# Channel loop of a gated attention and state-space kernel: short-lag sums moved to the step after their DRAM skew write, vector work reordered

## Chip, cores and metric

One core of a Trainium2 chip runs the whole program: the forward pass and all gradients of one layer. The metric is device microseconds for one execution, the median of several runs. Engines by short name: PE (matrix), DVE (vector), ACT (scalar), POOL (GpSimd) and SP, whose queue issues every DMA of this kernel. Each engine works through its own instructions in order and waits on semaphores for the others.

## Reference

The layer mixes two branches of a token sequence `x` (2048 tokens, 576 channels) with a gate of one number per token:

```python
g = _sigmoid((x * gate_w).sum(-1, keepdims=True))
a = _A_ref(x, A_wqkv, A_wo)                 # attention, 32 heads
b = _B_ref(x, B_A_re, ..., B_Dskip)         # state-space convolution
return g * a + (1 - g) * b
```

The second branch convolves every channel with a kernel of its own, made of 128 complex exponentials (shortened):

```python
logdA = dt * A                              # [D, N]
P = jnp.exp(logdA[:, :, None] * l[None, None, :])
K = jnp.einsum("dn,dnl,dn->dl", Cc, P, dB).real
y = irfft(rfft(u, 2L) * rfft(K, 2L))[:L] + u * Dskip
```

What is returned is the output and the gradients to all inputs, of which the state-space parameters need sums over all pairs of tokens by lag.

## The kernel before

**Stages.** The first 240 us project queries, keys and values; then comes attention with its gradients; from 2500 us the output projections' gradients; from 2890 to 4304 us the *channel loop*, the only part that changes; the last 175 us assemble outputs.

**Channel loop.** 576 channels are taken in 18 blocks of 32 (`CB`), each in two halves of 16 (`GS`). A sequence of 2048 is cut into 16 chunks (`NB`) of 128 positions. A step `i` of the loop works on several blocks at once: it prepares block `i+1`, scans and finishes block `i`, computes the close part of the convolution for block `i-1`, and in a side chain makes the short-lag sums of block `i+2`. The pieces, by the names used below:

- `ex`: on ACT, the exponential of the decay (tile `ab`), from a `phase` matmul on PE. `kk`, `ff`, `sn`: the angle. `kk` rounds the phase on ACT (the rounding pieces, four to a half), `ff` on DVE (L871) takes the fraction, `sn` makes three ACT passes of sine and square over a half. `prod` (L884, L885) multiplies on DVE to the tile `E1e`, and SP transposes it by DMA into `E1n`.
- `uv`: 32 matmuls with `E1e` against `RX`, the block's columns of input and gradient; ACT copies four pieces to `UV`. `RX` is loaded and scaled for two blocks at a time (`load_rx`, `prep_rx`), in even steps.
- `scan` (L910 to L920): 14 dependent steps of three DVE operations each on the chunk states `HG`; `casts` copies them on ACT; `rw1` (L936) and `rw2` (L942, L943) scale them into `Rw`; `ybp` is 64 matmuls from `Rw` to the far part of the output, copied by ACT to `ydi`, and the first column of the convolution kernel to `K0c`.
- `kp`: PE transposes `K0c`, ACT casts it, SP writes it to `Kp_d` in DRAM. `t0`, a step later: `T0w` reads it back as shifted copies (one buffer, 512 KB), 16 matmuls give `tps` in PSUM, and `tps` plus `ydi` is the output tile `yd`.
- `pairs` (L975 to L993): products of `UV` with the states on DVE, combined to three pairs of `rr` (one buffer), each pair added up by 30 or 28 matmuls against an identity; `sums` copies the result from the PSUM tile `misc`.
- Short-lag sums: `m_load` loads `xs` and `gyp` and makes seven copies of `xs` shifted by partitions; `m_mask` (L797, L799) masks them on DVE; `m_part` multiplies on PE into `psM` (one PSUM buffer that `tps` shares) and ACT copies to `mst`, which SP writes to `Md_d` in DRAM; `m_sum` reads `Md_d` back askew into `skw` (two buffers, four loads a block) and adds up on PE; `m_fin` copies to `RX`.

**What sets the order.** On PE, ACT, DVE and POOL the instructions stand as the loop's Python text emits them, call after call (a manual schedule). SP's DMAs are placed by the framework's scheduler, so that SP's order is seen in the built program. The phase matmuls have three PSUM buffers, `kk` one buffer, `RX` and `UV` two.

Of the kernel before, what the change touches and what calls it, by code (L numbers as in the profile page):

```python
# [20 lines left out]
def build(tc, aps, dbg_aps=None, stages=("s1", "attn", "post", "s4", "final")):  # L21
# [39 lines left out]
    with ExitStack() as gctx:  # L61
# [646 lines left out]
        if "s4" in stages:  # L708
# [13 lines left out]
            with ExitStack() as ctx:  # L722
# [37 lines left out]
                for u in range(2):  # L760
                    m_u = pc.tile([P, 4, MW], F32, name=f"mst{u}")
                    nc.vector.memset(m_u[:, :, P:MW], 0.0)
                    mst2.append(m_u)
                misc = pps.tile([P, 512], F32, tag="misc", name="misc")
# [180 lines left out]
                def ybp(b, h):  # L945
                    B_ = blk(b)
                    if h == 0:
                        B_["ydi"] = pw.tile([P, 2 * NS, CB], F32, tag="ydi", name="ydi")
                        B_["K0c"] = pw.tile([P, CB], F32, tag="K0c", bufs=2, name="K0c")
# [8 lines left out]
                    nc.scalar.copy(B_["ydi"][:, :, hs], yp[:, 1:, :])  # L958
# [9 lines left out]
                def pairs(b):  # L968
                    B_ = blk(b)
                    UV, hR, gR = B_["UV"], B_["hR"], B_["gR"]  # L970
                    pq = [pw.tile([P, 2, 2, 2, NS, CB], BF, tag=tg, name="pq") for tg in ("wA", "wB")]
                    pA, pB, pC, pD = pq[0][:, 0], pq[0][:, 1], pq[1][:, 0], pq[1][:, 1]

                    def pr(o, a_, hh):
                        nc.vector.tensor_tensor(o.rearrange("p a b n c -> p a b (n c)"),  # L975
                                                a_.rearrange("p b n c -> p b (n c)").unsqueeze(1).to_broadcast([P, 2, 2, NS * CB]),
                                                hh.rearrange("p a n c -> p a (n c)").unsqueeze(2).to_broadcast([P, 2, 2, NS * CB]), op=A.mult)

                    pr(pA, UV[:, :, CV0:CV0 + NS, :], hR)
                    pr(pB, UV[:, :, CV1:CV1 + NS, :], hR)  # L980
                    pr(pC, UV[:, :, CU1:CU1 + NS, :], gR)
# [3 lines left out]
                    nc.vector.tensor_tensor(pB, pB, pC, op=A.add)  # L985
                    for u, (pt_, n) in enumerate(((pA, NS), (pB, NS), (pD, NS - 1))):
                        rr = pw.tile([P, 2, NS, CB], BF, tag="rr", name="rr")
                        nc.vector.tensor_tensor(rr[:, 0, 0:n], pt_[:, 0, 0, 0:n], pt_[:, 1, 1, 0:n], op=A.subtract)
                        nc.vector.tensor_tensor(rr[:, 1, 0:n], pt_[:, 0, 1, 0:n], pt_[:, 1, 0, 0:n], op=A.add)
                        for ri in range(2):  # L990
                            o = (2 * u + ri) * CB
                            for k in range(n):
                                mm(misc[:, o:o + CB], lhsT=ident_bf, rhs=rr[:, ri, k, :], start=(k == 0), stop=(k == n - 1))  # L993
# [4 lines left out]
                def t0(b, h):  # L998
# [14 lines left out]
                    nc.scalar.copy(yd[:, :, 0, o0:o0 + GS], tps[:, :, 0, :])  # L1013
                    ydi = B_["ydi"].rearrange("p (a k) c -> p a k c", a=2)
                    nc.vector.tensor_tensor(yd[:, :, 1:NB, o0:o0 + GS], tps[:, :, 1:NB, :], ydi[:, :, :, h * GS:(h + 1) * GS], op=A.add)
# [11 lines left out]
                m_part(0, 1)  # L1027
                m_sum(0)
                m_fin(0)
                for i in range(-1, NBLK + 1):  # L1030
                    cur = 0 <= i < NBLK
                    nx = i + 1 < NBLK
                    mb = i + 2 if 1 <= i + 2 < NBLK else None
# [4 lines left out]
                    if cur:  # L1038
                        scan(i, 0, 4)
                    if nx:  # L1040
                        ff(i + 1, 0, 0); kk(i + 1, 0, 2)
                    if cur:
                        scan(i, 4, 7)
                    if nx:
                        ff(i + 1, 0, 1); kk(i + 1, 0, 3)
                    if cur:
                        scan(i, 7, 10)
                    if nx:
                        ff(i + 1, 0, 2)
                    if cur:  # L1050
                        scan(i, 10, 12)
# [15 lines left out]
                    if mb is not None and mb % 2 == 0:  # L1067
                        load_rx(mb // 2)
# [235 lines left out]
```

## Time and profile before

| what | us |
|---|---|
| runs: median of 3 (lowest, highest) | 4484.52 (4476.69, 4487.67) |
| the profiled execution | 4480.74 |
| its span | 4479.0 |
| attention and gradients, 240 to 2500: PE busy | 2214.8 of 2260 |
| channel loop, 2890 to 4304: DVE, ACT, PE busy | 834.4, 596.3, 518.4 of 1414 |
| `HG` cast (L910), once a step: first and last start | 2969.7, 4248.0 |

The profile is of one execution. A row of its timeline has the start and duration in us, the engine, the line, the operation, the tiles (out, then in), a count, and in brackets the engine's idle time before the row with what ended it. A row of the waits has the engine and line that waited, the engine and tile waited for, and then the total in us, the number of times and the longest. Where a helper emits an instruction (`mm`, L30), the line is the helper's, and the tile tells the place.

### The profile page before, as it was taken

The numbers are of one execution on the slowest core, as the hardware profiler recorded it, in microseconds if no ns is written. First come the engines' busy times: TensorE is split into PE (matmuls) and PEld (weight loads), VectorE is DVE, ScalarE is ACT, GpSimd is POOL, SyncE is SP. The second block draws the span as 40 slices with busy tenths as digits, with TensorE's granted clock in tenths as the row PEclk, the third lists the DMA queues.
The fourth block names the chain that finished last, engine by engine and source line by source line (L and its number), as shares of the span: only waits on it lengthen the run. The fifth ranks groups of instructions, "written<-read, shape, count | busy, mean of one in ns | idle before, by whom it ended". The sixth has DMA issues, their size and how long they took to land. (4 is left out here: it accounts for less than half of the span.)

```text
span 4479.0 us, 64906 instructions
## 1 busy us (share of the span) xinstructions
PE 3291.8 (73%) x24562; PEld 1166.9 (26%) x24562; DVE 2927.3 (65%) x5146; ACT 2933.1 (65%) x5376; POOL 21.8 (0%) x45
## 2 busy tenths in 40 slices
PE   8889999999999999999999987833343333343411
PEld 2312222222222222222222223522222222232300
DVE  5437777777677777776777771155656566565668
ACT  5379989899899898998998951154444444444401
POOL 0000000000000000000000000000000000000000
PEclk9855555555555555555555558955555555555555
DMA  7446777777776767777667777643443334243337
GB/s 195 137 111 118 126 136 122 133 129 124 138 120 126 135 122 132 129 125 136 121 122 127 121 146 210 147 80 74 73 79 71 77 66 88 56 82 71 69 114 170
DMA packets 1789270, 521.42 MB, mean 116 GB/s; under 512 B 1702074, under 2 KB 1767684, under 8 KB 1788956
## 3 DMA queue, kind: packets, MB, share of 16 engines
q1 hardware_dynamic: 1788956, 517.27, 59.5%
q8 instruction: 193, 3.16, 0.3%
q14 instruction: 121, 0.99, 0.1%
HBM read 102.10 MB, written 60.96 MB: 36 GB/s over the span
## 5 line engine op out<-in xcount | busy, mean ns | idle before, releaser
L604 DVE TENSOR_TENSOR ds<-ps_P,PT 128x512 bf16<-128x512 f32 x2048 | 1329.6, 687 | 467.7 <-PE ps_P L30 262.6
L595 ACT ACTIVATE PT<-ps_P 128x512 bf16<-128x512 f32 x2048 | 1226.3, 603 | 138.2 <-PE ps_P L30 86.3
L599 ACT ACTIVATE eb<-ps_P 128x512 bf16<-128x512 f32 x2048 | 1237.0, 606 | 19.9 <-PE ps_P L30 19.3
L30 PE MATMUL ps_P<-dOaT,VaT_g 19*128 19x512 bf16 x2048 | 1197.7, 601 | 26.6 <-DMA VaT_g<-VaT_d 25.7
L30 PE MATMUL ps_P<-KaT_g,QaT_g 19*128 19x512 bf16 x2048 | 1166.1, 594 | 7.6 <-ACT PT L595 7.6
L30 PE MATMUL ps_P<-QaT_g,KaT_g 19*128 19x512 bf16 x2048 | 1054.1, 615 | 9.8 <-DMA KaT_g<-KaT_d 5.8
L30 PE MATMUL accO<-PT,Vtok_g 128*32 128x512 bf16 x2048 | 331.5, 631 | 0.0
L30 PE MATMUL accK<-dsT,Qtok_g 128*32 128x256 bf16 x4096 | 315.2, 406 | 1.7 <-DVE dqa L481 0.8
L30 PEld LDWEIGHTS <-KaT_g 19*128 19x128 bf16 x2048 | 135.6, 103 | 690.6 <-issue 664.8
L30 PEld LDWEIGHTS <-VaT_g 19*128 19x128 bf16 x2048 | 197.3, 98 | 434.2 <-issue 404.8
L30 PE MATMUL psM<-xs,gyp 128*32 128x128 bf16 x576 | 42.3, 423 | 339.4 <-DVE xs L799 322.0
L30 PE MATMUL accQ<-ds,Ktok_g 128*32 128x512 bf16 x2048 | 266.9, 620 | 1.2 <-DVE dvacc L464 1.2
L30 PE MATMUL accV<-eb,dOa 128*32 128x512 bf16 x2048 | 266.9, 620 | 0.6 <-DVE dkacc L505 0.6
L871 DVE SCALAR_TENSOR_TENSOR kk<-kk,ph 128x512 f32<-128x512 f32 x144 | 95.1, 684 | 249.5 <-ACT kk L866 249.5
L30 PE MATMUL uvp<-RX,E1e 128*128 128x64 bf16 x1152 | 134.1, 290 | 111.9 <-DVE E1e L885 111.9
L30 PE MATMUL ph<-thr,lrow 3*128 3x512 bf16 x288 | 147.4, 591 | 64.0 <-DVE kk L871 20.7
L30 PEld LDWEIGHTS <-QaT_g 19*128 19x128 bf16 x2048 | 179.0, 100 | 51.6 <-issue 28.0
L481 DVE TENSOR_TENSOR dqa<-dqa,accQ 128x512 f32<-128x512 f32 x224 | 153.8, 687 | 48.9 <-PE accQ L30 48.6
L877 ACT ACTIVATE uk<-kk 128x2048 f32<-128x2048 f32 x36 | 68.8, 1911 | 176.0 <-DVE kk L871 175.9
L903 ACT ACTIVATE UV<-uvp 128x512 bf16<-128x512 f32 x144 | 86.0, 597 | 144.0 <-PE uvp L30 143.8
L464 DVE TENSOR_TENSOR dvacc<-dvacc,accV 128x512 f32<-128x512 f32 x224 | 154.0, 688 | 37.1 <-PE accV L30 19.5
L30 PE MATMUL ybp<-Rw,E1n 128*128 128x31 bf16 x1152 | 72.7, 233 | 134.8 <-ACT ydi L958 94.5
(279 smaller groups left out, 3641.4 us busy)
## 6 DMA issues: line engine op xcount, KB each, us to landing
T0w<-Kp_d SPq DMA_DIRECT2D x36, 512.0 KB
dsT<-ds SPq DMA_TRANSPOSE x512
dqkv_d<-dtk SPq DMA_DIRECT2D x96, 72.0 KB
dqkv_tok<-dqkv_d SPq DMA_DIRECT2D x1, 6912.0 KB
Md_d<-mst SPq DMA_DIRECT2D x144, 36.0 KB
ga_d<-ga_st SPq DMA_DIRECT2D x16, 288.0 KB
dxm_d<-dxm SPq DMA_DIRECT2D x16, 288.0 KB
skw<-Md_d SPq DMA_DIRECT2D x72, 64.0 KB
```

Source lines behind the costliest of these rows:

```text
L30: return nc.tensor.matmul(out, lhsT=lhsT, rhs=rhs, start=start, stop=stop, **kw)
L464: nc.vector.tensor_tensor(a_, a_, acc, op=A.add)
L481: nc.vector.tensor_tensor(U["dqa"], U["dqa"], acc, op=A.add)
L595: nc.scalar.activation(U["PT"][i][:, j, :], ps, ACT.Exp)
L599: nc.scalar.activation(e, ps, ACT.Exp)
L604: nc.vector.tensor_tensor(U["ds"][i][:, j, :], ps, U["PT"][i][:, j, :], op=A.mult)
L871: nc.vector.scalar_tensor_tensor(v_, v_, MAGIC, B_["ph"].pop((h, q)), op0=A.subtract, op1=A.subtract)
L877: nc.scalar.activation(uk, f_, ACT.Sin, scale=0.5 * TWO_PI * SIN_SAFE)
L903: nc.scalar.mul(UV[:, ri, :, c0:c0 + 8], pr, -1.0 if ri == 0 else 1.0)
```

## The change

Five things move; the arithmetic is the same.

1. The side chain of short-lag sums is one step longer. In step `i`, loading, masking and `m_part` are for block `i+3` (`mb`), and `m_sum` with `m_fin` is for block `i+2` (`sb`), whose `Md_d` was written at the end of the step before. Masks stand between the first half's `ybp` work and the second half's products; `m_part` is the last call of a step. Block 1's loading, masks and `m_part` come ahead of the loop.
2. `pairs` is split. `pairs1` (one product, its `rr`) stays; `pairs2` (the other products and sums) follows the second half's `uv`. `rr` has two buffers.
3. `rw1` follows `casts` directly, both `t0` halves come after it, `prep_rx` moves from a step's end to the place behind `t0`; the scan is dealt out as 2, 2, 2, 2 and 6 steps around the `ff`.
4. The third rounding piece of the second half is emitted ahead of `uv`; the fourth comes after the first `ff`, and `rw2` ahead of all four.
5. `ydi` becomes one tile, `ydi0`, with a zero column in front, so that one DVE addition writes `yd` and ACT's copy of column 0 goes.

```diff
+                ydi0 = pc.tile([P, 2, NB, CB], F32, name="ydi0")
+                nc.vector.memset(ydi0[:, :, 0, :], 0.0)
...
-                    nc.scalar.copy(B_["ydi"][:, :, hs], yp[:, 1:, :])
+                    nc.scalar.copy(ydi0[:, :, 1:NB, hs], yp[:, 1:, :].rearrange("p (a k) c -> p a k c", a=2))
...
+                def psum(u, pt_, n):
+                    rr = pw.tile([P, 2, NS, CB], BF, tag="rr", bufs=2, name="rr")
...
+                def pairs1(b):
...
+                    pmul(pq[0][:, 0], UV[:, :, CV0:CV0 + NS, :], hR)
+                    psum(0, pq[0][:, 0], NS)
+
+                def pairs2(b):
...
+                    pmul(pB, UV[:, :, CV1:CV1 + NS, :], hR)
+                    pmul(pC, UV[:, :, CU1:CU1 + NS, :], gR)
+                    nc.vector.tensor_tensor(pB, pB, pC, op=A.add)
+                    psum(1, pB, NS)
...
+                    psum(2, pD, NS - 1)
...
-                    nc.scalar.copy(yd[:, :, 0, o0:o0 + GS], tps[:, :, 0, :])
-                    ydi = B_["ydi"].rearrange("p (a k) c -> p a k c", a=2)
-                    nc.vector.tensor_tensor(yd[:, :, 1:NB, o0:o0 + GS], tps[:, :, 1:NB, :], ydi[:, :, :, h * GS:(h + 1) * GS], op=A.add)
+                    nc.vector.tensor_tensor(yd[:, :, :, o0:o0 + GS], tps, ydi0[:, :, :, h * GS:(h + 1) * GS], op=A.add)
...
+                m_load(1)
+                m_mask(1)
                 m_sum(0)
                 m_fin(0)
+                m_part(1, 0)
+                m_part(1, 1)
                 for i in range(-1, NBLK + 1):
...
-                    mb = i + 2 if 1 <= i + 2 < NBLK else None
+                    mb = i + 3 if i + 3 < NBLK else None
+                    sb = i + 2 if i + 2 < NBLK else None
...
                     if cur:
-                        scan(i, 12, 15)
+                        scan(i, 9, 15)
                         casts(i)
+                        rw1(i)
+                    if sb is not None and sb % 2 == 0:
+                        load_rx(sb // 2)
                     if i >= 1:
                         t0(i - 1, 0)
-                    if mb is not None:
-                        m_mask(mb)
-                        m_part(mb, 0)
-                    if i >= 1:
                         t0(i - 1, 1)
-                    if mb is not None:
-                        m_part(mb, 1)
...
+                    if sb is not None and sb % 2 == 0:
+                        prep_rx(sb // 2)
                     if nx:
                         prod(i + 1, 0)
-                        kk(i + 1, 1, 0); kk(i + 1, 1, 1)
+                        kk(i + 1, 1, 0); kk(i + 1, 1, 1); kk(i + 1, 1, 2)
                         uv(i + 1, 0)
-                    if cur:
-                        rw1(i)
-                    if nx:
-                        ff(i + 1, 1, 0); kk(i + 1, 1, 2)
-                        ff(i + 1, 1, 1); kk(i + 1, 1, 3)
                     if cur:
                         rw2(i)
                     if nx:
+                        ff(i + 1, 1, 0); kk(i + 1, 1, 3)
+                        ff(i + 1, 1, 1)
...
-                        pairs(i)
+                        pairs1(i)
                         kp(i)
+                    if mb is not None:
+                        m_mask(mb)
                     if nx:
                         prod(i + 1, 1)
                         uv(i + 1, 1)
                     if cur:
-                        sums(i)
-                    if mb is not None:
-                        if mb % 2 == 0:
-                            prep_rx(mb // 2)
-                        m_sum(mb)
-                        m_fin(mb)
+                        pairs2(i)
+                    if sb is not None:
+                        m_sum(sb)
+                        m_fin(sb)
                     if i + 2 < NBLK:
                         ex(i + 2, 0)
                         ex(i + 2, 1)
+                    if cur:
+                        sums(i)
+                    if mb is not None:
+                        m_part(mb, 0)
+                        m_part(mb, 1)
```

On **DVE**, in the middle of a step, from the last scan operation to `rw2`, before:

```order
L920 TENSOR_TENSOR HG<-tz 128x4x32
L1015 TENSOR_TENSOR yd<-tps,ydi 128x2x15x16
L797 TENSOR_TENSOR gyp<-gyp,omp 128x512
L799 TENSOR_SCALAR xs<-xs,msk 128x512 x7
L1015 TENSOR_TENSOR yd<-tps,ydi 128x2x15x16
L884 TENSOR_TENSOR E1e<-kk,ab 128x16x128
L885 SCALAR_TENSOR_TENSOR E1e<-uk,ab 128x16x128
L936 TENSOR_TENSOR wa<-HG,par 128x1920
L936 TENSOR_TENSOR wb<-HG,par 128x1920
L871 SCALAR_TENSOR_TENSOR kk<-kk,ph 128x512 x2
L942 TENSOR_TENSOR Rw<-wb,wa 128x960
L943 SCALAR_TENSOR_TENSOR Rw<-wa,wb 128x960
```

and after, in an even step, from the same operation to the `ff`:

```order
L922 TENSOR_TENSOR HG<-tz 128x4x32
L938 TENSOR_TENSOR wa<-HG,par 128x1920
L938 TENSOR_TENSOR wb<-HG,par 128x1920
L1022 TENSOR_TENSOR yd<-tps,ydi_39429 128x32x16 x2
L786 TENSOR_TENSOR RX<-gob,omg_t 128x1024
L788 TENSOR_SCALAR RX<-RX,l1col 128x960
L789 TENSOR_SCALAR RX<-RX,l0col 128x960
L886 TENSOR_TENSOR E1e<-kk,ab 128x16x128
L887 SCALAR_TENSOR_TENSOR E1e<-uk,ab 128x16x128
L944 TENSOR_TENSOR Rw<-wb,wa 128x960
L945 SCALAR_TENSOR_TENSOR Rw<-wa,wb 128x960
L873 SCALAR_TENSOR_TENSOR kk<-kk,ph 128x512 x4
```

The scalings `wa` and `wb` stand ahead of both `yd`, the masks have left this place, `prep_rx` (L786 to L789) has come in ahead of the products, and all four `ff` (L873) follow `rw2`.

On **ACT**, at the end of a step, from the last `UV` pieces of the second half to the first rounding pieces of the next step, before:

```order
L903 ACTIVATE UV<-uvp 128x64x8 x4
L996 COPY SS<-misc 128x6x32
L832 CAST RX<-misc 128x32
L833 ACTIVATE RX<-misc,l0col 128x32
L834 COPY dDs_row<-misc 1x32
L859 ACT_TABLE_LOAD
L859 ACTIVATE ab<-ph 128x512 x8
L866 ACTIVATE kk<-ph,magc 128x512 x4
```

and after:

```order
L905 ACTIVATE UV<-uvp 128x64x8 x4
L834 CAST RX<-misc 128x32
L835 ACTIVATE RX<-misc,l0col 128x32
L836 COPY dDs_row<-misc 1x32
L861 ACT_TABLE_LOAD
L861 ACTIVATE ab<-ph 128x512 x8
L1005 COPY SS<-misc 128x6x32
L812 COPY mst_39425<-psM 128x4x128
L812 COPY mst_39427<-psM 128x4x128
L868 ACTIVATE kk<-ph,magc 128x512 x4
```

`SS` has moved behind the exponentials (`ab`), and the two `mst` copies, which stood in the middle of the step, now come between these and the rounding pieces (`kk`).

On **SP**, from the `Kp_d` write of a block, before:

```order
L966 DMA Kp_d<-KT 32x128
L1008 DMA T0w<-Kp_d 128x16x128
L887 DMA_TRANSPOSE E1n<-E1e 128x32x128
L825 DMA skw<-Md_d 128x1x128 x2
L845 DMA thr<-spl_d 3x2048
L1008 DMA T0w<-Kp_d 128x16x128
L845 DMA thr<-spl_d 3x2048
```

and after, from the second transpose:

```order
L889 DMA_TRANSPOSE E1n<-E1e 128x32x128
L967 DMA Kp_d<-KT 32x128
L1017 DMA T0w<-Kp_d 128x16x128
L827 DMA skw<-Md_d 128x1x128 x2
L815 DMA Md_d<-mst_39425 16x4x144 x4
L815 DMA Md_d<-mst_39427 16x4x144 x4
L793 DMA xs<-in_A_x_dram 128x16x32
L794 DMA gyp<-in_grad_out_dram 128x16x32
L1017 DMA T0w<-Kp_d 128x16x128
L796 DMA xs<-xs 127x512
```

The transpose of the second half now precedes the `Kp_d` write and the first `T0w` load; the two `skw` loads still come behind all three, and the `Md_d` writes, the loads of `xs` and `gyp` and the second `T0w` follow them. The other two `skw` loads of a block stand behind the seven `xs` shifts (here the first of them is the last row).

More of the change, by code (lines that the diff above doesn't have):

```diff
@@ new lines, in psum @@
+                def psum(u, pt_, n):
+                    rr = pw.tile([P, 2, NS, CB], BF, tag="rr", bufs=2, name="rr")
+                    nc.vector.tensor_tensor(rr[:, 0, 0:n], pt_[:, 0, 0, 0:n], pt_[:, 1, 1, 0:n], op=A.subtract)
+                    nc.vector.tensor_tensor(rr[:, 1, 0:n], pt_[:, 0, 1, 0:n], pt_[:, 1, 0, 0:n], op=A.add)
+                    for ri in range(2):
+                        o = (2 * u + ri) * CB
+                        for k in range(n):
+                            mm(misc[:, o:o + CB], lhsT=ident_bf, rhs=rr[:, ri, k, :], start=(k == 0), stop=(k == n - 1))
@@ L969, in pairs @@
+                def pairs1(b):
                     B_ = blk(b)
                     UV, hR, gR = B_["UV"], B_["hR"], B_["gR"]
[L971 to L977, printed above, removed]
@@ L984, in pairs @@
                                                 hR[:, ri, 1:NS, :].unsqueeze(1).to_broadcast([P, 2, NS - 1, CB]), op=A.mult)
[L985 to L993, printed above, removed]
+                    psum(2, pD, NS - 1)
                 def sums(b):
@@ L1038, in build @@
                     if cur:
-                        scan(i, 0, 4)
+                        scan(i, 0, 3)
                     if nx:
@@ L1042, in build @@
                     if cur:
-                        scan(i, 4, 7)
+                        scan(i, 3, 5)
                     if nx:
@@ L1046, in build @@
                     if cur:
-                        scan(i, 7, 10)
+                        scan(i, 5, 7)
                     if nx:
@@ L1050, in build @@
                     if cur:
-                        scan(i, 10, 12)
+                        scan(i, 7, 9)
                     if nx:
```

16 lines of the change are left out of this document (9 added, 7 removed).

## Prediction

> **What bounds the kernel now.** I read the page first (its 40 slices and the granted clock), then a table of windows by stage, then the waits inside the channel loop, then the timeline of two neighbouring steps. The change touches the loop alone, and nothing else in the span of 4479.0 us moves.
>
> ```profile
> span 4479.0 us, 64906 instructions
> 2890.00:4304.00 1414.00, 518.43 (x5490) 356.53 (x5490) 834.41 (x1502) 596.31 (x881) 0.22 (x1) 0.52 0.38 72
> 3583.80:3662.30 78.50, 29.13 (x306) 19.96 (x305) 47.02 (x85) 33.21 (x50) 0.00 (x0) 0.50 0.42 79
> 3662.30:3737.70 75.40, 28.98 (x305) 19.88 (x305) 45.08 (x81) 33.13 (x50) 0.00 (x0) 0.50 0.35 69
> ```
>
> The columns are PE, PEld, DVE, ACT and POOL busy, granted clock, DMA share and GB/s. The loop takes 1414 us. The last two rows are one even and one odd step, cut from the first `ff` (L871) of a step to the first of the next: 78.5 and 75.4 us, mean 76.95. No engine is busy for two thirds of a step (DVE 47 of 78.5), so a step is a chain of waits. Which waits:
>
> ```profile
> DVE kk L871 <- ACT kk L866: 228.2, 17, 16.1
> ACT RX L832 <- PE misc L30: 177.7, 17, 13.1
> PE misc L30 <- DMA skw<-Md_d: 140.9, 31, 10.4
> DVE yd L1015 <- ACT yd L1013: 125.4, 32, 4.7
> ```
>
> The first three are one chain at the end of a step: PE waits for a `skw` load, ACT for PE's short-lag sums, DVE for ACT's first rounding piece; DVE loses 228.2/17 = 13.4 us a step there. The fourth lies inside the step, and so do the waits for PE in the timeline below. The odd-even pair shares everything but `prep_rx`, so one step's DVE timeline will do. Call F the first `ff`, E the end of the second half's products (L885).
>
> ```profile
> 3583.79 0.69 DVE L871 SCALAR_TENSOR_TENSOR kk<-kk,ph 128x512 f32<-128x512 f32 x1 [12.05 <-ACT kk L866]
> 3584.40 0.42 DVE L916 TENSOR_TENSOR tz<-HG,par 128x256 f32<-128x256 f32 x1
> 3585.50 0.43 DVE L916 TENSOR_TENSOR tz<-HG,par 128x256 f32<-128x256 f32 x1
> 3602.70 0.66 DVE L1015 TENSOR_TENSOR yd<-tps,ydi 128x480 bf16<-128x480 f32 x1 [4.70 <-ACT yd L1013]
> 3603.88 1.92 DVE L799 TENSOR_SCALAR xs<-xs,msk 128x512 bf16<-128x512 bf16 x7
> 3609.06 0.66 DVE L1015 TENSOR_TENSOR yd<-tps,ydi 128x480 bf16<-128x480 f32 x1 [3.26 <-ACT yd L1013]
> 3609.63 2.28 DVE L884 TENSOR_TENSOR E1e<-kk,ab 128x2048 bf16<-128x2048 f32 x1
> 3614.03 2.15 DVE L936 TENSOR_TENSOR wa<-HG,par 128x1920 f32<-128x1920 f32 x1
> 3622.69 2.23 DVE L975 TENSOR_TENSOR pq<-UV,hR 128x1920 bf16<-128x1920 bf16 x2
> 3631.81 0.41 DVE L988 TENSOR_TENSOR rr<-pq 128x480 bf16<-128x480 bf16 x1 [3.05 <-PE misc L30]
> 3633.28 0.39 DVE L988 TENSOR_TENSOR rr<-pq 128x448 bf16<-128x448 bf16 x1 [0.73 <-PE misc L30]
> 3633.89 2.29 DVE L884 TENSOR_TENSOR E1e<-kk,ab 128x2048 bf16<-128x2048 f32 x1
> 3638.29 1.22 DVE L784 TENSOR_TENSOR RX<-gob,omg_t 128x1024 bf16<-128x1024 bf16 x1
> 3662.27 0.69 DVE L871 SCALAR_TENSOR_TENSOR kk<-kk,ph 128x512 f32<-128x512 f32 x1 [15.89 <-ACT kk L866]
> ```
>
> Start-to-start differences are the prices: `ff` 0.60, a scan step 1.10, the two scalings (L936) 4.14, the masks 2.5 (L799 and 0.6 of L797 ahead of it), a pair product 1.07, an `rr` 0.35, the two product operations 4.4. Before, F to E is 3638.3 - 3583.8 = 54.5 us, and E to the next F 24.0 (even step) or 20.1 (odd, the 3583.79 row, whose E is 3563.7).
>
> **F to E after the change.** The rewritten DVE order, walked with those prices from F = 0: four `ff` and twelve scan steps (two now run ahead of F) end at 15.6; the scalings `rw1` follow directly and end at 19.8. The first `yd` then waits for nothing: its `tps` is long in PSUM, and it no longer passes through the ACT copy of column 0, which stood behind sines and casts; the 4.70 goes. The second waits only for PE's sixteen `tps` matmuls, about 1.4 where 3.26 stood; `yd` ends at 22.4. Products 26.8, `rw2` 28.9, three `ff` 30.7. The fourth `ff` is a new wait: ACT must copy four `UV` pieces before the last rounding piece, and they come from PE only after the products (3.72 of `uv` in the next fence, then the last copy and the rounding piece, 0.6 each), so it starts at 31.9 and ends at 32.5, 1.2 lost. Then `pairs1` (one product, two `rr`) 34.3, the masks 36.8, the second products 41.2. That is E in an odd step. In an even step `prep_rx` (1.9 us of DVE) now stands ahead of the first products, and its RX load waits on SP for the last `tps` (21.6 us): with 3.8 us for a load, 2 more are lost and E is 45.1; mean 43.2. So 11.3 us leave F to E, made up of three gone waits and of 5.6 us of pair work (two products, one sum, the rest) that now runs after E, under the end chain.
>
> **E to the next F.** The rows that price it:
>
> ```profile
> 3638.64 0.54 SPq L966 DMA_DIRECT2D Kp_d<-KT  x1
> 3644.73 0.39 SPq L1008 DMA_DIRECT2D T0w<-Kp_d  x1
> 3645.22 5.94 SPq L887 DMA_TRANSPOSE E1n<-E1e  x1
> 3573.47 1.53 SPq L825 DMA_DIRECT2D skw<-Md_d  x2
> 3576.13 1.26 PE L30 MATMUL misc<-sel,skw 128*128 128x8 f32 x4 [6.71 <-DMA skw<-Md_d]
> 3632.28 0.96 PE L30 MATMUL misc<-rr,ident_bf 128*128 128x32 bf16 x30 [0.50 <-DVE rr L988]
> 3638.43 3.72 PE L30 MATMUL uvp<-RX,E1e 128*128 128x64 bf16 x32 [3.59 <-DVE E1e L885]
> 3583.00 1.91 ACT L866 ACTIVATE kk<-ph,magc 128x512 f32<-128x512 f32 x3
> 3607.08 0.59 ACT L810 COPY mst<-psM 128x512 f32<-128x512 f32 x1 [4.41 <-PE psM L30]
> 3609.77 1.21 PE L30 MATMUL psM<-xs,gyp 128*32 128x128 bf16 x16 [0.97 <-DVE yd L1015]
> 4240.37 0.32 SPq L966 DMA_DIRECT2D Kp_d<-KT  x1
> 4241.78 0.37 SPq L1008 DMA_DIRECT2D T0w<-Kp_d  x1
> 4287.12 0.36 SPq L1008 DMA_DIRECT2D T0w<-Kp_d  x1
> 4291.06 1.09 PE L30 MATMUL tps<-RX,T0w 128*128 128x32 bf16 x16 [5.89 <-DMA T0w<-Kp_d]
> ```
>
> The step between the write of `Md_d` and its reading is meant to end the `skw` wait. But a block's sums need four `skw` loads and the tile still has two buffers: the second pair is issued only after PE has used the first, and in SP's order it stands behind the second transpose, the `Kp_d` write and a `T0w` load. Only the first pair gains the distance, and it was already early. Walk from E: transpose issue to 6.0; `Kp_d` lands 1.4 later (4240.37 to 4241.78, the last full products, where no `xs` shift is in flight), so `T0w` at 7.4 and the pair at about 7.9. PE gets there as late: the second `ybp`, which waits for an ACT copy behind the sines, then `psum` and the K transpose hold `uv` to 1.1; its 3.7, two groups of `psum` of 0.96, a wait of 0.1 and the first pair's 1.0 end at about 7.8. The pair lands 2.7 after issue when little is ahead (3573.47 to 3576.13), and PE would finish at 11.8; behind a `T0w` of 512 KB, which takes 3.9 (4287.12 to 4291.06), at 13 to 14. I take 13.2, near the upper end, since `T0w` is issued directly ahead. Then ACT: from the end of PE's sums (3577.4) to the old F (3583.79) were 6.4; now the `SS` copy, two `mst` copies and, between them, sixteen `psM` matmuls stand before the rounding piece: 0.2 + 0.5 + 1.3 + 0.6 = 2.6. E to F is 22.2, against a mean of 22.0 before. **The end chain does not get shorter**; the work moved under it is the gain.
>
> By the Trainium skill (DMA: Bandwidth & Descriptors, "Queues, rings and completion order"), each DMA engine consumes descriptors in ring order; that speaks against the new SP order, and by it alone the pair would end near 14, a step 0.8 longer; the trace's 2.7 is a case with the queue nearly empty.
>
> **Sum.** A step is 43.2 + 22.2 = 65.4 instead of 76.95: 11.55 saved. Steps 1 to 14 are full: 162. Step 0 has no `t0`: 5. Step 15 has no masks and no `psM` any more: 12. The last two steps, without the end chain: 11.5 less the 2 by which pair work outlasts `UV`, plus the 4 of the two `yd` waits, 14. The start loses: block 1's shifts and masks now precede the first `ff`.
>
> ```profile
> 2934.10 1.88 DVE L871 SCALAR_TENSOR_TENSOR kk<-kk,ph 128x512 f32<-128x512 f32 x3 [17.37 <-ACT kk L866]
> 2945.33 0.82 DVE L799 TENSOR_SCALAR xs<-xs,msk 128x512 bf16<-128x512 bf16 x2 [2.30 <-DMA xs<-xs]
> ```
>
> That is 2946.1 - 2934.1 = 12 us. In all 162 + 5 + 12 + 14 - 12 = 181 us. The profiled execution took 4480.74 (span 4479.0 and 1.7 around it), 0.1% under the median of 4484.52; a measurement of this kernel tells about 0.3% from no change. 4480.7 - 181 = **4300 us**. Cheap edits: the `memset` of `ydi0`, the `yd` operation on 512 instead of 480 columns (0.04 us, 36 times), and the four ACT copies of column 0 that go; under 2 us together.
>
> **Rivals.** (a) *The end wait goes as meant*: if the second pair were as early as the first, PE's sums would end at E + 8.8, and 16 steps save 4.4 more: 4230. SP's order and the two buffers speak against it. (b) *The `Kp_d` write lands late*, 6.1 us after issue (3638.64 to 3644.73) and not 1.4: `T0w` and the pair behind it come 4.7 later in 16 steps, 4375. That row has seven `xs` shifts directly ahead; in the new order these are issued some 25 us earlier, and only the transpose stands ahead. The same time would come out if half of what leaves F to E came back as waits I don't see. By the Trainium skill (the same page, "Why a DMA increments its semaphore by 16 and not by 1"), a transfer over 127 partitions runs on one DMA engine, so a write spread over sixteen must queue behind it there; that agrees with 6.1 against 1.4, and by it (b) would need the shifts in flight. (c) *Masks late, slower than before*: DVE now stops at the masks with the second products, the pair sums and the scan behind them. Their data come late in a chain on SP: `psM` of the step before, eight `Md_d` writes, `xs`, `gyp`, `T0w`, seven shifts.
>
> ```profile
> 3628.95 9.59 SPq L794 DMA_DIRECT2D xs<-xs  x7
> ```
>
> The shifts are issued from F + 5 and, overlapped, take 9.6 plus some 8 to land: about F + 23, needed at F + 34. Landing one after another, at 8 us each, they would be done only at F + 61: each step 27 us longer than my 65.4, about 16 x 15.5 = 250 us slower than before, 4730. It decides against the kernel from F + 46 on. The row's seven issues in 9.6 us speak against it. (d) *Nothing gained*: the DVE waits come back in full elsewhere, 4480.
>
> **How the numbers follow.** Forecast 0.62, from 4265 to 4345 (the pair's landing between the two bounds, and 1.5 us a step in F to E); (a) 0.10; (b) 0.21; (c) 0.04; (d) 0.03. Faster by over 0.3% are the first three, 0.93; same 0.03; slower 0.04. The range reaches from (a) past (b): 4225 to 4400.
>
> **What would show it.** After: the wait of L912's `HG` gone or short, no DVE idle before the first `yd`, `rr` without the 3.05; PE still waiting for `skw` once a step with the *second* pair, 3 to 6 us; `ff` waiting on ACT 8 to 13 us; `Kp_d` to `T0w` under 2.5 us. Wrong would be: no `skw` wait (then a), `Kp_d` to `T0w` of 6 (b), masks waiting for shifts (c), an F to E mean outside 41 to 46.

## The result, and the profile after

| | before | after |
|---|---|---|
| median of 4 runs each (lowest, highest), us | 4484.84 (4476.69, 4487.67) | 4308.89 (4303.29, 4315.7) |
| the profiled execution, us | 4480.74 | 4303.29 |
| its span, us | 4479.0 | 4301.6 |

The ratio of the medians is 0.961, with a 95% interval from 0.9591 to 0.9632: 3.9% faster. The profiled execution took 177.4 us less, where 181 were predicted (4300 against 4303.29).

First the windows of the kernel after, with the same columns as before: PE, PEld, DVE, ACT and POOL busy, granted clock, DMA share, GB/s. The first row is the channel loop, the next two an even and an odd step.

```profile
2890.00:4126.00 1236.00, 491.84 (x5490) 350.67 (x5490) 836.69 (x1485) 593.51 (x845) 0.00 (x0) 0.57 0.45 82
3508.20:3575.40 67.20, 27.15 (x305) 19.41 (x305) 47.38 (x85) 33.10 (x48) 0.00 (x0) 0.59 0.52 92
3575.40:3638.10 62.70, 27.31 (x305) 19.52 (x305) 45.32 (x81) 32.97 (x48) 0.00 (x0) 0.55 0.43 83
```

The loop went from 1414 to 1236 us, which is the whole gain, with DVE and ACT as busy in total as before (836.7 and 593.5 against 834.4 and 596.3). What went is waiting. The longest waits of DVE, ACT and PE in the loop, and the one of SP for `Kp_d`, each with total, times and longest:

```profile
DVE kk L873 <- ACT kk L868: 260.2, 35, 15.2
ACT RX L834 <- PE misc L30: 143.5, 17, 9.6
PE misc L30 <- DMA skw<-Md_d: 87.7, 18, 6.2
SPq L1017 <- DMA Kp_d<-KT: 31.5, 17, 3.1
DVE yd L1022 <- PE tps L30: 19.7, 17, 1.2
DVE RX L788 <- DMA RX<-xr_d: 15.5, 7, 2.9
DVE HG L912 <- ACT UV L905: 4.4, 1, 4.4
DVE xs L801 <- DMA xs<-xs: 1.5, 1, 1.5
```

Three rows are the same chain as before: PE for `skw`, ACT for PE's sums, DVE for the first rounding piece. It is not gone. DVE's wait on ACT is even longer, 260.2 with 18 short ones of 1.1 in it, so some 14 us a step at the first `ff`, against 13.4. What is gone are waits inside a step. In the kernel before, DVE's list also had these two:

```profile
DVE HG L910 <- ACT UV L903: 64.9, 18, 4.5
DVE rr L988 <- PE misc L30: 64.0, 34, 3.1
```

Now no wait of `rr` for PE's pair sums is left, and the 125.4 for ACT's copy of column 0 has become 19.7, for PE; both stood between F and E. The `HG` cast's wait (now 4.4, once) stood behind E, where DVE waits for the first rounding piece anyway, so that its going saves nothing by itself. The masks waited 1.5 us in the whole loop.

DVE's timeline, columns as before, shows the first `ff` of blocks 0, 2, 16 and 17 (F), and between them the odd step 9, which starts with the first `ff` of block 10:

```profile
2944.07 1.28 DVE L873 SCALAR_TENSOR_TENSOR kk<-kk,ph 128x512 f32<-128x512 f32 x2 [5.26 <-ACT kk L868]
...
3051.03 0.69 DVE L873 SCALAR_TENSOR_TENSOR kk<-kk,ph 128x512 f32<-128x512 f32 x1 [13.98 <-ACT kk L868]
...
3575.36 0.69 DVE L873 SCALAR_TENSOR_TENSOR kk<-kk,ph 128x512 f32<-128x512 f32 x1 [13.88 <-ACT kk L868]
...
3594.87 0.68 DVE L1022 TENSOR_TENSOR yd<-tps,ydi 128x512 bf16<-128x512 f32 x1
3596.71 0.69 DVE L1022 TENSOR_TENSOR yd<-tps,ydi 128x512 bf16<-128x512 f32 x1 [1.16 <-PE tps L30]
...
3606.83 0.69 DVE L873 SCALAR_TENSOR_TENSOR kk<-kk,ph 128x512 f32<-128x512 f32 x1 [1.10 <-ACT kk L868]
...
3613.91 2.29 DVE L887 SCALAR_TENSOR_TENSOR E1e<-uk,ab 128x2048 bf16<-128x2048 f32 x1
...
3638.11 0.69 DVE L873 SCALAR_TENSOR_TENSOR kk<-kk,ph 128x512 f32<-128x512 f32 x1 [13.60 <-ACT kk L868]
...
3969.01 0.69 DVE L873 SCALAR_TENSOR_TENSOR kk<-kk,ph 128x512 f32<-128x512 f32 x1 [13.49 <-ACT kk L868]
...
4030.33 0.69 DVE L873 SCALAR_TENSOR_TENSOR kk<-kk,ph 128x512 f32<-128x512 f32 x1 [12.45 <-ACT kk L868]
```

F to E is now 3613.91 + 2.29 - 3575.36 = 40.8 us (predicted 41.2), and inside it DVE stands still only twice, 1.16 and 1.10, at the second `yd` and the fourth `ff` of the second half. E to the next F is 3638.11 - 3616.20 = 21.9 (predicted 22.2). Over steps 3 to 12, F to E is 42.9 on the mean and E to F 22.5, where 43.2 and 22.2 were predicted; before, they were 54.6 and 22.2. Where that time goes is in the timeline of SP, PE and ACT behind E = 3616.20:

```profile
3616.26 4.82 SPq L889 DMA_TRANSPOSE E1n<-E1e  x1
3621.17 0.54 SPq L967 DMA_DIRECT2D Kp_d<-KT  x1
3622.60 0.73 PE L30 MATMUL misc<-sel,skw 128*128 128x8 f32 x4
3623.11 0.39 SPq L1017 DMA_DIRECT2D T0w<-Kp_d  x1
3623.59 1.90 SPq L827 DMA_DIRECT2D skw<-Md_d  x2
3627.83 1.02 PE L30 MATMUL misc<-sel,skw 128*128 128x8 f32 x4 [4.50 <-DMA skw<-Md_d]
3628.89 0.18 ACT L834 CAST RX<-misc 128x32 bf16<-128x32 f32 x1 [8.00 <-PE misc L30]
...
3636.80 0.58 ACT L812 COPY mst<-psM 128x512 f32<-128x512 f32 x1 [1.24 <-PE psM L30]
3637.39 1.84 ACT L868 ACTIVATE kk<-ph,magc 128x512 f32<-128x512 f32 x3
```

PE has the first pair at E + 6.4 and then waits 4.50 us for the second, which SP issued at E + 7.4, behind the second transpose, the `Kp_d` write and a `T0w` load. PE's sums end at E + 12.7. This is the wait that the prediction said would stay, with its cause: two `skw` buffers for four loads.

The step shown is one of the short ones. From `Kp_d` to `T0w` are 1.7 to 2.0 us in ten steps of sixteen, and 3.5 to 3.7 in the other six (in the next step, 3688.01 to 3691.73); the second pair goes out that much later, and E to F is then 23.2 to 23.6 in five of these six, against 21.7 to 22.4 in nine of the ten.

### The profile page after: what moved, and what is told of

Same layout as the page of the kernel before. It is cut to its first block, busy times and chain, and to the rows that moved or that the text cites. A ratio compares the mean times of both kernels' runs of the same rounds, so it can differ in the third digit from the quotient of the medians.

```text
span 4301.6 us, 64847 instructions
## 1 busy us (share of the span) xinstructions
PE 3258.9 (76%) x24562; PEld 1164.5 (27%) x24562; DVE 2930.2 (68%) x5147; ACT 2930.2 (68%) x5340; POOL 21.7 (1%) x45
## 5 line engine op out<-in xcount | busy, mean ns | idle before, releaser
L599 ACT ACTIVATE eb<-ps_P 128x512 bf16<-128x512 f32 x2048 | 1240.0, 607 | 19.8 <-PE ps_P L30 19.4
L30 PE MATMUL tps<-RX,T0w 128*128 128x32 bf16 x576 | 38.5, 234 | 314.9 <-DVE yd L1022 301.7
L873 DVE SCALAR_TENSOR_TENSOR kk<-kk,ph 128x512 f32<-128x512 f32 x144 | 95.1, 683 | 265.6 <-ACT kk L868 265.6
L868 ACT ACTIVATE kk<-ph,magc 128x512 f32<-128x512 f32 x144 | 91.1, 688 | 147.7 <-DVE E1e L886 144.1
L30 PEld LDWEIGHTS <-E1e 128*128 128x128 bf16 x1152 | 126.2, 123 | 145.8 <-DVE E1e L887 144.7
```

The lines of the kernel that those rows point to most:

```text
L30: return nc.tensor.matmul(out, lhsT=lhsT, rhs=rhs, start=start, stop=stop, **kw)
L599: nc.scalar.activation(e, ps, ACT.Exp)
L868: nc.scalar.activation(B_["kk"][h][:, 4 * q:4 * q + 4, :], ph, ACT.Identity, bias=magc, scale=1.0)
L873: nc.vector.scalar_tensor_tensor(v_, v_, MAGIC, B_["ph"].pop((h, q)), op0=A.subtract, op1=A.subtract)
```

## Experiments

Each kernel was timed in three rounds beside the kernel before; ratios below are to it. "After" was 0.9611. E to F means from the end of the second half's products to the next first `ff`, taken from the middle steps of each trace.

**Are the two buffers the bound?** The kernel after, with four:

```diff
-                        skw = pw.tile([P, P], F32, tag="skw", bufs=2, name="skw")
+                        skw = pw.tile([P, P], F32, tag="skw", bufs=4, name="skw")
```

> The changed kernel with four skw buffers instead of two. Theory (the end of a step still waits for the second pair of skw loads, because the tile has two buffers): all four loads go out behind the xs shifts, PE makes the sums at E+6.4 to E+8.2 without waiting, E to the next F falls from 22.6 to about 17.2 us, 16 steps save 5.4 each: about 4223 us. Rival (the move to the next step has already hidden the loads, and what ACT and DVE wait for at the end is PE and ACT work alone): no change, 4300 to 4315. Second rival (the T0w load and the transposes of the end, not skw, set the end): 4280 to 4300.

Measured: 4225.6, ratio 0.9425 (0.9411 to 0.9439), 83 us under the kernel after. SP's queue in its timeline, around a step whose E is 3638.2:

```profile
3608.09 2.65 SPq L827 DMA_DIRECT2D skw<-Md_d  x4
...
3638.26 4.87 SPq L889 DMA_TRANSPOSE E1n<-E1e  x1
3643.22 0.54 SPq L967 DMA_DIRECT2D Kp_d<-KT  x1
3646.71 0.39 SPq L1017 DMA_DIRECT2D T0w<-Kp_d  x1
```

All four loads are issued 30 us ahead of E. PE waits for no `skw` load any more, and DVE's wait at `ff` falls from 260.2 to:

```profile
DVE kk L873 <- ACT kk L868: 166.6, 35, 9.3
```

E to F falls from 22.5 to 17.1 us, F to E nearly stays (40.8 in odd and 46 in even steps, against 40.9 and 45). So the second pair was the wait that ended last, by some 5.5 us a step.

The same one number changed in the kernel *before*:

> The kernel before with four skw buffers and nothing else. Theory (same wait, two buffers, in the kernel before): the four loads go out together in the middle of a step, PE makes the sums at E+4.7 to E+6.7, E to F falls from 22.0 to about 13.1 us, 16 steps save 8.9: about 4343 us, three quarters of what the whole change brought. Rival (the short distance between the write of Md_d and its reading is the wait, as the description of the change has it): under 20 us saved, 4465 or more.

Measured: 4330.0, ratio 0.9664 (0.965 to 0.9679), 13 us under my theory. F to E is 54.6 as before; E to F falls from 22.2 on the mean to between 12.1 and 13.0. Its SP timeline around E = 3629.6 shows the loads behind the *first* half's transpose (issued at 3605.40), 19 us ahead of E:

```profile
3610.36 2.68 SPq L825 DMA_DIRECT2D skw<-Md_d  x4
```

Two more buffers of 64 KB take some 150 us off the kernel before, nearly as much as the whole change does, and by the other half of the step: the change shortened F to E and left E to F, this does the reverse.

**What the side chain's extra step gives.** In the kernel after, part 1 of the change undone: loading, masks and `m_part` at their old places, for the block whose sums follow in the same step.

```diff
-                m_load(1)
-                m_mask(1)
...
-                m_part(1, 0)
-                m_part(1, 1)
...
-                    mb = i + 3 if i + 3 < NBLK else None
+                    mb = i + 2 if 1 <= i + 2 < NBLK else None
...
                         t0(i - 1, 0)
+                    if mb is not None:
+                        m_mask(mb)
+                        m_part(mb, 0)
+                    if i >= 1:
                         t0(i - 1, 1)
+                    if mb is not None:
+                        m_part(mb, 1)
...
-                    if mb is not None:
-                        m_mask(mb)
...
-                    if mb is not None:
-                        m_part(mb, 0)
-                        m_part(mb, 1)
```

> The changed kernel with the side chain of short-lag sums (loading, masks, psM, sums) put back to the step and places it had before, all else as changed. Theory (the longer distance is not what gained): masks cost DVE the same 2.5 us in either place, the two mst copies leave the end chain (2.6 us less), but psM and tps share a buffer again (some 2 us of DVE wait) and the xs shifts stand ahead of the Kp_d write again (2 to 4 us more at the end): a step is 1 to 4 us longer, 4325 to 4375 us. Rival (the distance is the gain): most of the 177 us are lost, 4430 or more.

Measured: 4418.4, ratio 0.986 (0.9845 to 0.9875), 110 us over the kernel after: 43 us above the range of my theory and 12 short of the rival's. F to E is 44.9 in odd and 48.7 in even steps (4.0 more on the mean), E to F 27.8 to 28.7 and 24.5 to 25.2 in turn (4.0 more). SP's timeline of a step with E = 3678.2:

```profile
3674.64 3.69 SPq L796 DMA_DIRECT2D xs<-xs  x4
3678.45 8.60 SPq L889 DMA_TRANSPOSE E1n<-E1e  x1
3687.16 0.52 SPq L967 DMA_DIRECT2D Kp_d<-KT  x1
3687.73 2.66 SPq L796 DMA_DIRECT2D xs<-xs  x3
3691.21 0.40 SPq L1017 DMA_DIRECT2D T0w<-Kp_d  x1
3691.74 4.55 SPq L827 DMA_DIRECT2D skw<-Md_d  x2
```

The `xs` shifts stand at the step's end again: four are issued directly ahead of the transpose, whose issue takes 8.60 instead of 4.82, three between `Kp_d` and `T0w`, and the second pair goes out at E + 13.5 instead of E + 7.4. In every other step no shift stands directly ahead of the transpose, and its issue takes 4.9 to 5.6; these are the steps with the shorter E to F. Between F and E of the step shown, DVE has two waits that are longer than in the kernel after:

```profile
3658.91 0.69 DVE L1022 TENSOR_TENSOR yd<-tps,ydi 128x512 bf16<-128x512 f32 x1 [3.03 <-PE tps L30]
3673.67 2.29 DVE L886 TENSOR_TENSOR E1e<-kk,ab 128x2048 bf16<-128x2048 f32 x1 [2.09 <-ACT kk L880]
```

The second `yd` waits 3.03 instead of 1.16, with the matmuls of `psM` between the two `tps` halves again; the second half's products wait 2.09 for ACT's sines, a time that the masks fill in the kernel after. Together they are the 4.0 of F to E; my theory had only the first. So part 1 acts through the order of instructions on SP and DVE.

Part 1 alone, in the kernel before:

```diff
+                m_load(1)
+                m_mask(1)
                 m_sum(0)
                 m_fin(0)
+                m_part(1, 0)
+                m_part(1, 1)
...
+                    if mb is not None:
+                        m_mask(mb)
                     if nx:
                         prod(i + 1, 1)
...
+                    if mb is not None:
+                        m_part(mb, 0)
+                        m_part(mb, 1)
```

> The kernel before with the move of the side chain alone (loading, masks and psM for block i+3, sums a step after the write). Theory: F to E falls by 2 us (no psM between the tps halves); the xs shifts no longer stand ahead of the Kp_d write, so T0w, the transpose and the second skw pair go out some 5 us earlier, against 2.6 us for psM and mst at the end; a step is about 72 us instead of 76.95, the start 10 us longer: about 4410 us. PE still waits for the second skw pair. Rival (the distance is the gain): no skw wait any more, about 4340. Second rival (the move alone is worth nothing, all the gain is the order on DVE): 4470 to 4490.

Measured: 4417.4, ratio 0.986 (0.9843 to 0.9876), near my 4410. F to E is 52.7, E to F 18.4 to 19.4. SP's and PE's rows around E = 3679.9:

```profile
3674.09 0.31 SPq L966 DMA_DIRECT2D Kp_d<-KT  x1
3675.44 0.38 SPq L1008 DMA_DIRECT2D T0w<-Kp_d  x1
3679.96 5.63 SPq L887 DMA_TRANSPOSE E1n<-E1e  x1
3685.69 1.31 SPq L825 DMA_DIRECT2D skw<-Md_d  x2
3688.20 0.60 PE L30 MATMUL misc<-sel,skw 128*128 128x8 f32 x2 [2.60 <-DMA skw<-Md_d]
```

With the shifts out of the way and E as late as before, `Kp_d` and `T0w` go out *ahead* of the transpose, and the second pair is used from E + 8.3. Here the end chain did get shorter, by some 3 us.

To tell the distance from the order: part 1 undone as above, with four buffers.

> The side chain undone as in the run before, but with four skw buffers. Theory (what the longer distance is worth is only the place of the xs shifts, Kp_d and T0w ahead of the second skw pair; with four buffers no load stands in the end chain): E to F about 14.6 us (no mst copies there), F to E as in that run 46.8 on the mean, a step 61.4: about 4240 us, 15 us from the changed kernel with four buffers (4225.6). Rival (the distance matters by itself, since loads a step after the write land in time and loads in the same step do not): PE waits for skw, 4300 or more.

Measured: 4215.9, ratio 0.9413 (0.9399 to 0.9427), 24 us under my theory. E to F is 14.1 to 14.7, F to E 44.9 and 48.7. PE waits for no `skw` load: the four go out 8 to 9 us ahead of E, without the distance, and are in time. So with four buffers the distance is worth nothing, and what part 1 still does is to change the order: against the kernel after with four buffers, F to E is 3.5 us longer (the same two waits) and E to F 2.9 shorter (no `psM` and `mst` copies there). From the first `ff` of block 0 to that of block 17 it takes 1012.7 us against 999.4. That it is some 10 us faster all the same (4225.6 to 4215.9) comes from the start, which my theory left out: without block 1's early loading and masks the first `ff` of block 0 comes at 2931.3 instead of 2953.6.

**What the split of the pairs gives.** In the kernel after, `pairs2` directly behind `pairs1`:

```diff
                         pairs1(i)
+                        pairs2(i)
                         kp(i)
...
-                    if cur:
-                        pairs2(i)
```

> The changed kernel with all pair sums back ahead of the second half's products (pairs2 directly behind pairs1). Theory (the pair work was hidden under the end chain by the split): 5.6 us of DVE work return ahead of E, F to E about 48 us instead of 42.9 on the mean; the end chain is set by SP's second skw pair and stays at 22 us: about 4395 us. Rival (the split only changes the order of work that is on the path either way): 4300 to 4325.

Measured: 4372.7, ratio 0.9765 (0.975 to 0.978), 64 us over the kernel after, between theory and rival. F to E is 48.8 and 52.9, 8 us more: beside the 5.6 of work that I had counted, `rr` waits for PE's pair sums again (34.9 us in 17 times, 2.1 a step). E to F is 18.1 to 19.4, on the mean 18.5 and 4 less, where I had expected it to stay at 22. SP's timeline around E = 3665.0 has the reason:

```profile
3659.39 0.31 SPq L967 DMA_DIRECT2D Kp_d<-KT  x1
3660.74 0.39 SPq L1017 DMA_DIRECT2D T0w<-Kp_d  x1
3665.07 4.84 SPq L889 DMA_TRANSPOSE E1n<-E1e  x1
3670.00 1.32 SPq L827 DMA_DIRECT2D skw<-Md_d  x2
```

With E later, `Kp_d` and `T0w` get out ahead of the transpose again and the second pair at E + 5. So the split takes 8 us out of F to E and gives half back behind E. In the kernel after, ACT's cast that makes the data of `Kp_d` ends at 3617.01, 0.8 us behind E, and SP's order has the transpose first; here it ends at 3659.37, 5.7 us ahead of E, and SP's order has `Kp_d` first. That the scheduler chose these orders for this reason is likely but not shown.

**`rw1` and the copy of column 0.** `rw1` back beside `rw2`; and, on top of that, the ACT copy back:

```diff
                         casts(i)
-                        rw1(i)
...
                     if cur:
+                        rw1(i)
                         rw2(i)
```

> The changed kernel with rw1 (4.1 us of DVE) back behind uv, next to rw2. Theory (yd has no wait left that rw1 would have to cover, since its ACT copy is gone; products and UV come 4 us earlier, which ends the new 1.2 us wait of the fourth ff): 0 to 1.2 us less a step, 4285 to 4310 us. Rival (rw1 covers the wait of yd for ACT or PE): 3 to 5 us more a step, 4360 to 4390 us.

Measured: 4309.2, ratio 0.9621 (0.9607 to 0.9635): no difference from 0.9611. F to E is 39.9 in odd steps and 46.7 in even ones, against 40.8 and about 45: what odd steps gain, even ones lose to the `RX` load, whose wait grows from 15.5 to 34.8 us.

```diff
-                    nc.vector.tensor_tensor(yd[:, :, :, o0:o0 + GS], tps, ydi0[:, :, :, h * GS:(h + 1) * GS], op=A.add)
+                    nc.scalar.copy(yd[:, :, 0, o0:o0 + GS], tps[:, :, 0, :])
+                    nc.vector.tensor_tensor(yd[:, :, 1:NB, o0:o0 + GS], tps[:, :, 1:NB, :], ydi0[:, :, 1:NB, h * GS:(h + 1) * GS], op=A.add)
```

> The changed kernel with rw1 back next to rw2 and with the ACT copy of column 0 restored in front of each addition to yd. Theory (either of the two would have ended the first yd's wait of 4.7 us; with neither, yd stands behind sines and casts on ACT again): F to E 2.5 to 4 us longer than with rw1 back alone, about 4350 to 4370 us. Rival (the copy is cheap and its place does not matter): within 10 us of that run (4309).

Measured: 4339.1, ratio 0.9686 (0.9672 to 0.9701), 30 us over the kernel without the copy: less than my theory, more than the rival. F to E is 42.5 in odd steps, 2.6 more, and 47.1 in even ones, 0.4 more. The waits of its DVE:

```profile
DVE yd L1023 <- ACT yd L1022: 63.8, 34, 2.4
DVE RX L788 <- DMA RX<-xr_d: 18.4, 7, 3.3
```

That is 1.9 us on the mean for each of 34 additions, half of the 3.9 (125.4/32) of the kernel before. In a step it is 2.4 for the first, which had no wait without the copy, and 1.4 for the second, which had 1.2. In even steps the wait for `RX` hides most of it: that fell from 34.8 to 18.4.

**How far it goes.** Three more steps on top of four buffers. `m_part`, and with it `m_load`, behind the next step's first rounding pieces, so that `psM` and `mst` no longer stand ahead of them:

```diff
-                    if mb is not None:
-                        m_load(mb)
...
                         kk(i + 1, 0, 0); kk(i + 1, 0, 1)
+                    if sb is not None and sb >= 1:
+                        m_part(sb, 0)
...
                         ff(i + 1, 0, 0); kk(i + 1, 0, 2)
+                    if sb is not None and sb >= 1:
+                        m_part(sb, 1)
+                    if mb is not None:
+                        m_load(mb)
...
-                    if mb is not None:
-                        m_part(mb, 0)
-                        m_part(mb, 1)
```

> The changed kernel with four skw buffers, and m_part (psM and the two mst copies) moved behind the first two rounding pieces of the next step. Theory (the two copies and the psM between them stand in the end chain with 2.6 us, and ACT has room for them behind F): E to F falls from 17.0 to about 14.6 us, F to E stays: about 4188 us. Rival (the copies only take the place of another wait, or come back as waits of the later rounding pieces): 4215 to 4235.

Measured: 4200.0, ratio 0.9373 (0.9358 to 0.9389), between theory and rival. E to F is 14.1 to 14.9, some 3 us less as expected, but even steps lose most of it: F to E is 49, since the `RX` load now goes out some 3 us later and DVE waits 45.4 us for it in seven steps, 6.5 each. So `prep_rx` went to the step's end, behind `pairs2`:

```diff
-                    if sb is not None and sb % 2 == 0:
-                        prep_rx(sb // 2)
...
                         pairs2(i)
                     if sb is not None:
+                        if sb % 2 == 0:
+                            prep_rx(sb // 2)
                         m_sum(sb)
```

> The kernel of the last run but one (four skw buffers, psM late), with prep_rx moved from the place behind the tps additions to behind the last pair sums, where it stood in the kernel before. Theory (in even steps prep_rx costs its 1.9 us of DVE and a wait for the RX load, 8 us together in that run, and DVE has 4 to 6 us idle at the step's end): F to E of even steps falls from 49 to about 41 us, E to F stays near 14.1, seven or eight steps save 8: about 4140 us. Rival (the operations only move into the end chain, since PE or ACT wait for RX there): 4185 to 4205.

Measured: 4139.8, ratio 0.9239 (0.9224 to 0.9255), as expected: F to E is 40.9 in even steps too, and E to F 14.1 to 15.0. With `rw1` beside `rw2` as well:

> As the run before it, with rw1 back next to rw2 as well. Theory (products and UV 4 us earlier, the fourth ff no longer waits): 1 us a step less than the run before, about 4125 us. Rival (no difference, as the earlier run with rw1 back had none): equal to the run before within 10 us.

Measured: 4129.9 (4124.0 to 4135.2), ratio 0.922 (0.9203 to 0.9238). Its interval overlaps with that of the kernel ahead of it, so `rw1`'s place stays without a shown effect; either of the two beats both the kernel before and the one after, the last by 4%.

## Why the prediction held

**The sum.** By the first `ff` rows of both traces. Before, block 0 had it at 2934.10, and blocks 2, 16 and 17 here:

```profile
3048.60 0.69 DVE L871 SCALAR_TENSOR_TENSOR kk<-kk,ph 128x512 f32<-128x512 f32 x1 [14.11 <-ACT kk L866]
...
4123.33 0.69 DVE L871 SCALAR_TENSOR_TENSOR kk<-kk,ph 128x512 f32<-128x512 f32 x1 [14.92 <-ACT kk L866]
...
4193.30 0.69 DVE L871 SCALAR_TENSOR_TENSOR kk<-kk,ph 128x512 f32<-128x512 f32 x1 [7.39 <-ACT kk L866]
```

| term | predicted, us | measured, us |
|---|---|---|
| start: first `ff` of block 0 | -12 | 2934.1 - 2944.1 = -10.0 |
| the rest up to step 1 (block 0's step, step 0) | 5 | (3048.6 - 2934.1) - (3051.0 - 2944.1) = 7.6 |
| steps 1 to 14 | 162 | 1074.7 - 918.0 = 156.7 |
| step 15 | 12 | 70.0 - 61.3 = 8.7 |
| from the last first `ff` to the end | 14 | 285.7 - 271.3 = 14.4 |
| all | 181 | 177.4 |

A step from 1 to 14 takes 918.0/14 = 65.6 us where 65.4 was predicted, against 76.8 before. No term is off by more than 5.3, and the errors have both signs, so that some of the nearness of 177.4 to 181 is luck.

**F to E.** Each wait went as walked: none at the first `yd`, 1.16 at the second (1.4 predicted), 1.10 at the fourth `ff` (1.2), 2.2 (15.5/7) for `RX` in an even step (2). The copy of column 0 is shown by its return: 30 us, with `rw1` beside `rw2`; with `rw1` ahead of `yd`, as in the kernel after, its return was not tried.

**E to F, and what went wrong in the reading of it.** The step "the end chain does not get shorter; the work moved under it is the gain" is right as a total, and the second pair's wait for a buffer is shown by both runs with four. But the unchanged 22 us is a balance. The means over steps 3 to 12 of four traces show it:

| kernel | F to E, us | E to F, us |
|---|---|---|
| before | 54.6 | 22.2 |
| part 1 alone | 52.7 | 18.9 |
| all but part 1 | 46.9 | 26.6 |
| after | 42.9 | 22.5 |

Part 1 takes the shifts out of SP's queue at the step's end, and E to F gets 3 to 4 us shorter. The other parts make it some 4 us longer: with the split, E comes ahead of the data of `Kp_d`, and the transpose stands ahead of `Kp_d`, `T0w` and the pair (E to F is 18.5 with the pairs whole). The prediction took SP's new order as given and walked it rightly, but it did not see that this order costs something; and the going of the shifts was in it as the price of `Kp_d`'s landing (1.4 for 6.1, rival (b)), not as a gain of part 1. "Only the first pair gains the distance" is true of the distance, but part 1 was worth 110 us in the kernel after.

The expectation for its undoing, 4325 to 4375 against 4418.4, failed by two terms. It put the shifts at 2 to 4 us; E to F grew by 4.0 although `psM` and `mst` had left it, which is 2.9 by the runs with four buffers, so that SP's order is worth some 7 (an estimate). And it missed the 2.1 that the second half's products wait for the sines. Two signs of the prediction failed as well: DVE's wait at `ff` was forecast as 8 to 13 us and is some 14, and `Kp_d` to `T0w` was to be under 2.5 us, which holds in ten steps of sixteen.

The parts don't add up: part 1 alone in the kernel before gives 65 us, everything but part 1 gives 64 (both against 4482.6, the median of the kernel before beside them), and both together 177. By the table, E to F adds up within 0.8 us. Most of the difference is in F to E, where part 1 saves 1.9 alone and 4.0 with the others: the wait for the sines, which the masks fill at their new place, is there only in the new order on DVE.

**The rivals.** (a), the wait gone: it stands at 87.7/18 = 4.9 us. Its price, 70 us, was near the 83 that came once the buffers were there. (b), `Kp_d` landing 6.1 us late: in the step shown `T0w` follows it after 3623.11 - 3621.17 = 1.9, against 1.4 in the sum, with the shifts far ahead, from F + 5.5. In six steps of sixteen it is 3.5 to 3.7 without any shift near, so part of (b) came true there. (c), masks late: 1.5 us once. (d), all waits back elsewhere: F to E fell by 11.7 us and E to F grew by 0.3.

By the Trainium skill (DMA: Bandwidth & Descriptors, "Queues, rings and completion order") each DMA engine consumes descriptors in ring order; the second pair behind `T0w` was used 3627.83 - 3623.59 = 4.2 us after its issue, against 2.7 with little ahead, which agrees in direction. PE's sums ended at E + 12.7, 1.3 us ahead of the 14 that the prediction gave for that rule.

Left open: the fourth part (the order of the rounding pieces and `rw2`) and the new places of `t0` were not tried alone. Nor was that of `prep_rx` in the kernel after, where even steps have an F to E 4.1 us longer than odd ones; in the later kernel with four buffers, its move back gained 60 us (4200.0 to 4139.8).

## What to carry to other kernels

When a wait for a load ends last, count the buffers of its tile against the loads it needs before looking at when its data are written: here two more buffers in the kernel before did by one number nearly what the whole reordering did. Follow the issuing queue's order for every move, also of instructions that seem unrelated: here shifts that left the place ahead of a critical load were worth more than the longer distance between write and read, and where DVE's products ended earlier, their transpose stood ahead of a write that had been in front. Work moved under an unchanged wait counts only as far as that wait does not move with it.

## What the hardware showed that was not expected

- How long a small write takes to land depends on what stands ahead of it on SP. `Kp_d` to `T0w` took 5.9 to 6.2 us in nearly all steps of the kernel before, with seven shifts issued just ahead. Directly behind the transpose, in the kernel after, it took 1.7 to 2.0 or 3.5 to 3.7. Ahead of the transpose, with part 1 alone or the pairs whole, it was 1.3 to 1.4 in most steps. What tells the 1.9 from the 3.6 was not found.
- Issuing one and the same transpose took SP 4.8 to 5.8 us in the middle of the loop where the queue had stood idle just before. It took 8.3 to 8.6 directly behind `xs` shifts (part 1 undone), 7.8 to 8.2 behind them in the same kernel with four buffers, and as much, 7.8 to 8.1, directly behind the write of `yd_d` in the last kernel: it is not the shifts alone. All behind it in the queue waits as long.
- The granted clock in the loop rose from 0.52 to 0.57 and PE's busy time for the same 5490 matmuls fell from 518.4 to 491.8 us. It is not PE's share alone: the kernel before with four buffers has PE busy for 331.5 of the 800 us from 3100 at 0.52 to 0.53, the kernel after for 334.3 at 0.56 to 0.58. What sets it apart was not tried.
